# First group's products and masks by chunk, keys and scores in tiles of their own, and other orders in the opening and the first three turns

## The chip, the cores and the metric

The kernel runs on one core of one Trainium2 chip. The metric is the device time of one execution in microseconds (us), the median of several runs. Lower is better. A profile of one execution gives the times of single instructions.

## The reference, cut to what matters

```python
# gated linear attention: B, H, S, D = 4, 8, 768, 48
for t in range(S):
    state = alpha[:, :, t, :, None] * state + k[:, :, t] (outer) v[:, :, t]
    y[:, :, t] = q[:, :, t] @ state
x = y as (B, S, H*D)                                  # 4 x 768 x 384
# gated state-space block: d_inner = 512
proj = x @ w_in                                       # 384 x 1024
val, gate = proj[..., :512], proj[..., 512:]
h_t = a * h_(t-1) + val_t                             # a = exp(A_log), a scan over time
out = (silu(gate) * h) @ w_out                        # 512 x 384
```

The weights w_in and w_out arrive as 64-bit floats and are converted to 32-bit on the chip. q, k, v and alpha are 32-bit.

## The kernel before, in words

The sequence is cut into N = 12 groups of 256 steps (three for each of four batches). A group has two chunks (`c`) of 128 steps, and a chunk two halves of L = 64 steps; `u` counts the four blocks of 64. The order of all instructions is written out by hand (no scheduler): each engine, and each queue that issues DMAs, works its own list from front to back and waits for others by semaphores.

The attention of a group `m` goes in these steps:

- Products. alpha, q and k of the group are brought to a layout with the 48 dimensions on the partitions: for groups 0 to 2 by TensorE (`alphas`, `straighten`: 16 matmuls with the identity, and a ScalarE copy from PSUM, L648, L658, L663), from group 3 on by VectorE (`turn`, L576). `scan_P` (L602) scans the running product P of alpha, `scan_V` (L610 to L618) scans V, the inverse product, backwards. `scaled_q` (L585) writes q times P into `Zq`, `scaled_k` (L590) writes k times V into `Zk`. From group 3 on these steps are the generator `products`, whose seven steps are taken by `go(1)` and `go(2)` in between the steps of a turn. `junk` (L596) is a check on ScalarE that reads alpha.
- `scores(m)` (L684): for each half and head, one matmul of `Zk` against `Zq`. `Zq` holds the identity in its first 48 columns, so that the result has 48 columns that give the key back, by steps, and 64 columns that are scores. Chunk 0 goes to the PSUM tile `s`, chunk 1 to a tile `mm`.
- `masks(m)`: ScalarE copies the keys from PSUM into `AK` (L693; for one half of the heads the scores too), VectorE multiplies scores by the triangular mask into the same `AK` (L699), and GpSimd masks the other half (L696). For group 0 (`alone`) all four masks are VectorE's.
- `values(m)` (L714) multiplies the masked scores with v, `states(m)` (L741) the keys with v. ScalarE copies the states to `dS` (L746), GpSimd adds them up (`add_up`, L756 and L758, tile `sum`), and `carried` (L727) adds the part of earlier blocks to the PSUM tile `y`. For group 0 `carried_by_parts` (L767) does that from `dS` directly.
- `join(m)`: ScalarE copies `y` to `yst` (L788), eight DMAs move it to the rows of `xT` (L790), and two copies move the rest (L793).

The state-space block of a group `n` goes in `project(n, cc)` for cc = 0 to 3 (L806, six matmuls of 128x256 columns, VectorE's scan `hh` L809, ScalarE's `sg` L814, GpSimd's product `f` L815), and `output(n)` (L824, L828, L829). `convert(i)` makes 32-bit weights of the 64-bit ones, for i = 0 to 3 a quarter of w_in, for 4 and 5 a half of w_out: ScalarE's `low` (L525) and three VectorE operations (L534, L536, L538). `load_w` and `load_w_out` load the 64-bit weights.

The loop runs over turns n = 0 to 11. In turn n the state-space block of group n and the attention of group m = n + 1 are interleaved, and the products of group n + 2 go on VectorE. `first` is scores and masks, `second` is values, states and sums, `third` is the carried part, the other half of the values, and `join`. Pools matter: PSUM tiles `mm` come from a pool of two (projections, scores of chunk 1, outputs and transposes take turns), `s` and `y` have one each. `keep_warm` issues matmuls on zeros without a use for the result.

Of the kernel before, what the change touches and what calls it, by code (L numbers as in the profile page):

```python
# [345 lines left out]
def fast(  # L346
# [68 lines left out]
    def load_steps(name, m, engine):  # L415
# [49 lines left out]
    AK = [const.tile([C, G, 4, L + D], FP32, name=f"AK{i}") for i in range(2)]  # L465
    Zqs = [const.tile([C, 4, 2 * G, L + D], FP32, name=f"Zq{i}") for i in range(2)]
# [16 lines left out]
    def constants():  # L483
# [21 lines left out]
        for t in sums:  # L505
            nc.gpsimd.memset(t[:, :, D:64], 0.0)
        for t in Zqs:
            for i in range(2):
                rows = ds(64 * i, 64)
                nc.gpsimd.tensor_copy(out=t[rows, :, :, 0:D].rearrange("p h u d -> p (h u) d"),  # L510
# [69 lines left out]
    def plain(name):  # L580
        tag = "Zk" if name == "k" else "q"
        return (p2 if name == "k" else p1).tile([C, 4, GC], FP32, tag=tag, name=tag)

    def scaled_q(m, t, P):
        nc.vector.tensor_mul(Zqs[m % 2][:, :, :, D:], t.rearrange("p h (u t) -> p h u t", t=L),  # L585
                             P[:, :, 1:GP].rearrange("p h (u t) -> p h u t", t=L))

    def scaled_k(m, t, V):
        Zks[m] = t
        nc.vector.tensor_mul(t, t, V[:, :, 1:GP])  # L590

# [83 lines left out]
    def scores(m):  # L675
        Zk, Zq = Zks[m], Zqs[m % 2]
        scs[m] = [bank_pair("s"), bank_pair()]
        for c in range(G):
            for p in range(4):
                for h in range(2):  # L680
                    u = 2 * c + h
                    for i in range(2):
                        rows = ds(64 * i, D)
                        nc.tensor.matmul(scs[m][c][ds(L * h, L), i, ds(p * (L + D), L + D)],  # L684
                                         Zk[rows, p, ds(u * L, L)], Zq[rows, p, u],
                                         start=True, stop=True, skip_group_check=True)

    def masks(m, alone=False):
        sc = [t[:, :, 0:4 * (L + D)].rearrange("p i (h x) -> p i h x", h=4) for t in scs.pop(m)]
        for i in (1, 0):  # L690
            for c in range(G):
                n = L + D if i and not alone else D
                nc.scalar.activation(AK[i][:, c, :, 0:n], sc[c][:, i, :, 0:n], AF.Copy)  # L693
        if not alone:
            t = AK[1].rearrange("p c h x -> p (c h) x")[:, :, D:]
            nc.gpsimd.tensor_mul(t, t, mask[:, None, :].to_broadcast([C, G * 4, L]))  # L696
        for c in range(G):
            for i in range(2 if alone else 1):
                nc.vector.tensor_mul(AK[i][:, c, :, D:], sc[c][:, i, :, D:],  # L699
                                     mask[:, None, :].to_broadcast([C, 4, L]))  # L700

    def values(m, across):
# [4 lines left out]
        for c in range(G):  # L707
            for e in range(2):
                for h in range(2):
                    i = 1 - h if across else h  # L710
                    for s in range(2):
# [3 lines left out]
                                         v_sb[rows, c, 4 * i + p, :], AK[i][rows, c, p, D:],  # L715
# [303 lines left out]
```

## Time and profile before

| what | value |
|---|---|
| median of 3 runs | 299.87 us (298.01 to 300.7) |
| profiled execution, its own time | 299.45 us |
| its span | 297.6 us |
| TensorE matmul busy | 280.9 us (94%), 4062 instructions |
| VectorE busy | 210.3 us (71%) |
| ScalarE busy | 107.9 us (36%) |
| GpSimd busy | 118.4 us (40%) |
| mean granted TensorE clock | 0.98 |

PE is TensorE's matmul, PEld its weight load, DVE VectorE, ACT ScalarE, POOL GpSimd, SP SyncE, whose queue issues most DMAs. L12 is line 12 of the kernel. In the strips of the page the span is cut into 40 equal slices, and each digit is the busy share in tenths; PEclk is the clock that TensorE was granted, in tenths of full speed. A timeline row gives the start, the length, the engine, the line, the operation, the tiles, and in brackets the idle time before it with what ended it. The chain of waits is followed back from the last instruction.

### The profile page before, as it was taken

The numbers are of one execution on the slowest core, as the hardware profiler recorded it, in microseconds if no ns is written. First come the engines' busy times: TensorE is split into PE (matmuls) and PEld (weight loads), VectorE is DVE, ScalarE is ACT, GpSimd is POOL, SyncE is SP. The second block draws the span as 40 slices with busy tenths as digits, with TensorE's granted clock in tenths as the row PEclk, the third lists the DMA queues.
The fourth block names the chain that finished last, engine by engine and source line by source line (L and its number), as shares of the span: only waits on it lengthen the run. The fifth ranks groups of instructions, "written<-read, shape, count | busy, mean of one in ns | idle before, by whom it ended". The sixth has DMA issues, their size and how long they took to land.

```text
span 297.6 us, 9503 instructions
## 1 busy us (share of the span) xinstructions
PE 280.9 (94%) x4062; PEld 220.8 (74%) x4062; DVE 210.3 (71%) x233; ACT 107.9 (36%) x236; POOL 118.4 (40%) x139
## 2 busy tenths in 40 slices
PE   7997987879999999999999999999999999999991
PEld 5886876458868878778778688688687787786860
DVE  4879665948659959849859679598599598259420
ACT  1766446130532532433235144224315333331211
POOL 8001728314405626516318238146156174141110
PEclk9999998895999999999999999999999999999998
DMA  6990798634188197294394593791871921100101
GB/s 211 252 327 14 216 328 185 144 93 101 29 205 209 42 245 168 70 255 122 82 266 115 135 249 74 166 247 45 219 198 43 247 61 41 55 15 28 55 4 62
DMA packets 54180, 41.86 MB, mean 141 GB/s; under 512 B 29520, under 2 KB 52016, under 8 KB 54128
## 3 DMA queue, kind: packets, MB, share of 16 engines
q1 hardware_dynamic: 53184, 40.60, 52.5%
q8 instruction: 34, 0.56, 0.8%
q10 hardware_dynamic: 816, 0.40, 0.5%
q0 software_dynamic: 128, 0.16, 0.2%
q14 instruction: 18, 0.15, 0.2%
HBM read 32.88 MB, written 4.72 MB: 126 GB/s over the span
## 4 chain that ended last, share of the span: by engine, by line
PE 76%; DMA 6%; DVE 5%; POOL 4%; ACT 4%; issue 2%; SPq 1%; DVEq 0%; POOLq 0%; ACTq 0%
PE pvg L806 37%; PE o L824 18%; PE y L714 4%; PE y L727 4%; PE s L741 3%; PE mm L648 3%; PE s L684 3%; DMA wbits<-in_moe_w_in_dram 3%; POOL sum L758 3%; PE mm L684 2%; DMA raw_k<-in_k_dram 1%; DMA raw_a<-in_alpha_dram 1%; DVE hh L809 1%; POOL f L815 1%; ACT dS L746 1%
## 5 line engine op out<-in xcount | busy, mean ns | idle before, releaser
L806 PE MATMUL pvg<-xT,w_in 128*128 128x256 f32 x576 | 137.5, 393 | 1.0 <-DVE w_in L538 1.0
L806 PEld LDWEIGHTS pvg<-xT,w_in 128*128 128x128 f32 x576 | 109.1, 194 | 18.6 <-PE s L741 1.1
L815 POOL TENSOR_TENSOR f<-sg,hh 128x256 f32<-128x256 f32 x48 | 57.9, 1208 | 52.0 <-ACT sg L814 52.0
L824 PE MATMUL o<-w_out,f 128*128 128x384 f32 x192 | 64.4, 487 | 1.4 <-POOL f L815 0.8
L814 ACT ACTIVATE sg<-pvg 128x256 f32<-128x256 f32 x48 | 18.5, 385 | 112.3 <-DVE hh L809 88.5
L824 PEld LDWEIGHTS o<-w_out,f 128*128 128x128 f32 x192 | 36.5, 191 | 25.1 <-POOL f L815 1.4
L758 POOL TENSOR_TENSOR sum<-sum,dS 128x192 f32<-128x192 f32 x40 | 33.0, 824 | 28.7 <-ACT dS L746 26.8
L809 DVE TENSOR_TENSOR_SCAN hh<-a_dec,hh,pvg 128x256 f32<-128x256 f32 x32 | 23.2, 724 | 21.4 <-PE pvg L806 21.3
L696 POOL TENSOR_TENSOR AK<-AK,mask 128x512 f32<-128x512 f32 x11 | 14.0, 1272 | 57.9 <-ACT AK L693 57.9
L699 DVE TENSOR_TENSOR AK<-s,mask 128x256 f32<-128x256 f32 x13 | 5.4, 424 | 38.9 <-ACT AK L693 38.9
L602 DVE TENSOR_TENSOR_SCAN P<-al,lower 128x1028 f32<-128x1028 f32 x12 | 27.6, 2298 | 4.1 <-ACT al L658 4.0
L618 DVE TENSOR_TENSOR_SCAN V<-al,ends 128x1028 f32<-128x1028 f32 x12 | 27.9, 2328 | 0.1
L828 ACT ACTIVATE o_sb<-o 128x384 f32<-128x384 f32 x24 | 10.5, 488 | 47.0 <-PE o L824 47.0
L714 PE MATMUL y<-AK,v 64*64 64x64 f32 x768 | 16.9, 225 | 2.5 <-POOL AK L696 2.0
L714 PEld LDWEIGHTS y<-AK,v 64*64 64x64 f32 x768 | 14.0, 137 | 6.4 <-issue 4.2
L576 DVE STREAM_TRANSPOSE Zk<-raw_k 128x1024 f32<-128x1024 f32 x9 | 18.4, 2045 | 0.0
L576 DVE STREAM_TRANSPOSE al<-raw_a 128x1024 f32<-128x1024 f32 x9 | 18.4, 2042 | 0.0
L576 DVE STREAM_TRANSPOSE q<-raw_q 128x1024 f32<-128x1024 f32 x9 | 18.2, 2020 | 0.0
L727 PE MATMUL y<-Zq,sum 48*64 48x64 f32 x656 | 15.2, 223 | 1.8 <-issue 1.2
L727 PEld LDWEIGHTS y<-Zq,sum 48*64 48x64 f32 x656 | 12.3, 134 | 6.0 <-issue 3.7
L585 DVE TENSOR_TENSOR Zq<-q,P 128x1024 f32<-128x1024 f32 x12 | 14.7, 1221 | 0.4
L741 PE MATMUL s<-v,AK 64*64 64x48 f32 x704 | 14.2, 223 | 0.8 <-issue 0.8
(93 smaller groups left out, 274.0 us busy)
## 6 DMA issues: line engine op xcount, KB each, us to landing
v<-in_v_dram SPq DMA_DIRECT2D x24, 192.0 KB, 3.8
out_dram<-o_sb SPq DMA_DIRECT2D x24, 192.0 KB, 3.3
raw_a<-in_alpha_dram SPq DMA_DIRECT2D x18, 184.0 KB, 4.5
raw_k<-in_k_dram SPq DMA_DIRECT2D x18, 184.0 KB, 4.3
raw_q<-in_q_dram SPq DMA_DIRECT2D x18, 184.0 KB, 4.2
raw_a<-in_alpha_dram SPq DMA_DIRECT2D x18, 176.0 KB, 4.6
raw_k<-in_k_dram SPq DMA_DIRECT2D x18, 176.0 KB, 4.4
raw_q<-in_q_dram SPq DMA_DIRECT2D x18, 176.0 KB, 4.4
```

The costliest lines, as they stand in the source:

```text
L576: nc.vector.transpose(out=by_runs(to).rearrange("p h c j -> p h j c"), in_=raws[name][:, 0:4 * ROW].rearrange("p (h j d) -> p h j d", h=4, ...
L602: nc.vector.tensor_tensor_scan(out=P, data0=al[:, 0:4 * GP], data1=lower.rearrange("p h t -> p (h t)"), initial=0.0, op0=ALU.mult, op1=ALU ...
L618: nc.vector.tensor_tensor_scan(out=V[:, ::-1], data0=al[:, 1:4 * GP + 1][:, ::-1], data1=ends.rearrange("p h t -> p (h t)")[:, ::-1], init ...
L714: nc.tensor.matmul(ys[m][ds(64 * s, 64), i, e, ds(c * C + h * L, L)], v_sb[rows, c, 4 * i + p, :], AK[i][rows, c, p, D:], start=across and ...
L727: nc.tensor.matmul(ys[m][ds(64 * s, 64), i, e, ds(u * L, L)], Ss[j][rows, p, :], Zqs[m % 2][rows, p, u, D:], start=False, stop=True, skip_ ...
L741: nc.tensor.matmul(st[ds(64 * i, 64), h, c, p, :], AK[i][rows, c, p, 0:64], vs[m % NV][rows, c, 4 * i + p, 0:D], start=True, stop=True, sk ...
L758: nc.gpsimd.tensor_add(Ss[j][:, :, 0:D], Ss[j - 1][:, :, 0:D], part)
L806: nc.tensor.matmul(pj, w_ins[cc][:, kk, vg, :], xT[:, kk, :], start=(kk == 0), stop=(kk == NK - 1))
L809: nc.vector.tensor_tensor_scan(out=hh, data0=a_dec[:, cc:cc + 1].to_broadcast([C, GC]), data1=pv, initial=prev_h[cc][:, GC - 1:GC] if n % ...
L814: nc.scalar.activation(sg, pg, AF.Silu)
L815: return lambda: nc.gpsimd.tensor_mul(fs[n][:, cc, :], sg, hh)
L824: nc.tensor.matmul(os[c], fs[n][:, cc, ds(c * C, C)], w_outs[cc // 2][:, cc % 2, :], start=(cc == 0), stop=(cc == NI - 1))
```

## The change

Line numbers of the kernel after the change differ by some ten to twenty.

- `AK` becomes two kinds of tiles, `As` for masked scores and `Ks` for keys. `masks` copies keys and masks scores chunk by chunk, a key ahead of its score; for other groups than 0 GpSimd's half of the scores is copied first. `Ks` gets zeros in its last 16 columns from GpSimd at the start.
- `Zq` and `Zk` are laid out by chunk; k has a tile of its own from which `scaled_k` writes `Zk`. For group 0 `scaled_k` and `scaled_q` go chunk by chunk, behind `scan_V`.
- The first loads of alpha, q and k are split over SyncE's and ScalarE's queues. The second half of w_in is loaded ahead of the first scores instead of behind `join(0)`.
- Two of the zero matmuls are gone. In the opening, `scan_P(1)` stands behind the masks of group 0, `straighten(1, "k")` and `scan_V(1)` behind `join(0)`, `convert(0)` before it. `join(0)` issues its DMAs from GpSimd's and ScalarE's queues, and half of its copy is VectorE's.
- `straighten` of group 2 for k and q moves into turn 0, and `junk(2)` and the scans of group 2 move behind `convert(5)`.
- In turn 1, the first two projections stand before the scores; in turn 2, one projection. `carried` goes over blocks 0, 2, 3 in place of 2, 3, 0.

```diff
-            engine.dma_start(
+            engines[i % len(engines)].dma_start(
                 out=steps_of(name, m)[:, ds(i * ROW, ROW)],
...
-    AK = [const.tile([C, G, 4, L + D], FP32, name=f"AK{i}") for i in range(2)]
-    Zqs = [const.tile([C, 4, 2 * G, L + D], FP32, name=f"Zq{i}") for i in range(2)]
+    As = [const.tile([C, G, 4, L], FP32, name=f"A{i}") for i in range(2)]
+    Ks = [const.tile([C, G, 4, L], FP32, name=f"K{i}") for i in range(2)]
+    Zqs = [const.tile([C, 2 * G, 4, L + D], FP32, name=f"Zq{i}") for i in range(2)]
...
+    def scaled_q(m, t, P, c=None):
+        u0, n = (0, 2 * G) if c is None else (2 * c, 2)
+        at = ds(u0 * L, n * L)
+        nc.vector.tensor_mul(Zqs[m % 2][:, ds(u0, n), :, D:].rearrange("p u h t -> p h u t"),
...
+    def scaled_k(m, t, V, c=None):
+        if not c:
+            Zks[m] = p2.tile([C, G, 4, C], FP32, tag="Zk", name="Zk")
+        c0, n = (0, G) if c is None else (c, 1)
...
-        for i in (1, 0):
+        mb = mask[:, None, :]
+        if not alone:
             for c in range(G):
-                n = L + D if i and not alone else D
-                nc.scalar.activation(AK[i][:, c, :, 0:n], sc[c][:, i, :, 0:n], AF.Copy)
-        if not alone:
-            t = AK[1].rearrange("p c h x -> p (c h) x")[:, :, D:]
-            nc.gpsimd.tensor_mul(t, t, mask[:, None, :].to_broadcast([C, G * 4, L]))
+                nc.scalar.activation(As[1][:, c], sc[c][:, 1, :, D:], AF.Copy)
+            t = As[1].rearrange("p c h x -> p (c h) x")
+            nc.gpsimd.tensor_mul(t, t, mb.to_broadcast([C, G * 4, L]))
         for c in range(G):
-            for i in range(2 if alone else 1):
-                nc.vector.tensor_mul(AK[i][:, c, :, D:], sc[c][:, i, :, D:],
-                                     mask[:, None, :].to_broadcast([C, 4, L]))
+            for i in range(2):
+                nc.scalar.activation(Ks[i][:, c, :, 0:D], sc[c][:, i, :, 0:D], AF.Copy)
+                if alone or i == 0:
+                    nc.vector.tensor_mul(As[i][:, c], sc[c][:, i, :, D:], mb.to_broadcast([C, 4, L]))
...
-        for i in range(2):
-            nc.scalar.activation(st[:, i], y[:, i], AF.Copy)
+        nc.scalar.activation(st[:, 0], y[:, 0], AF.Copy)
+        if m == 0:
+            nc.vector.tensor_copy(out=st[:, 1], in_=y[:, 1])
+        else:
+            nc.scalar.activation(st[:, 1], y[:, 1], AF.Copy)
...
+    load_w(1, nc.sync)
     nc.scalar.activation(a_dec, a_log, AF.Exp)
     nc.scalar.activation(spare, minus, AF.Silu)
     P = scan_P(0)
-    scaled_q(0, tq, P)
     junk(0)
     V = scan_V(0, P)
-    scaled_k(0, tk, V)
-    keep_warm(2, 512)
+    for c in range(G):
+        scaled_k(0, tk, V, c)
+        scaled_q(0, tq, P, c)
     alphas(1)
     tq = straighten(1, "q", "y")
     junk(1)
     keep_warm(1, 512, "s")
     scores(0)
+    masks(0, True)
     P = scan_P(1)
-    masks(0, True)
-    tk = straighten(1, "k")
     low(0)
     values(0, True)
     states(0)
     low(1)
-    V = scan_V(1, P)
+    convert(0)
     carried_by_parts(0)
     values(0, False)
-    join(0, [nc.sync, nc.gpsimd])
+    join(0, [nc.gpsimd, nc.scalar])
+    tk = straighten(1, "k")
+    V = scan_V(1, P)
     scaled_q(1, tq, P)
     scaled_k(1, tk, V)
-    convert(0)
     convert(1)
-    load_w(1, nc.sync)
...
-    P = scan_P(2)
-    tk = straighten(2, "k")
-    tq = straighten(2, "q")
-    load_raw("a", 3, nc.sync)
-    load_v(2, nc.sync)
-    for name in "kq":
-        load_raw(name, 3, nc.sync)
...
-            carried(m, (2, 3, 0))
+            carried(m, (0, 2, 3))
...
             f1 = project(n, 1)
+            tk = straighten(2, "k")
+            load_raw("k", 3, nc.sync)
             second(m)
             f0()
             f1()
             convert(3)
-            junk(2)
             f2 = project(n, 2)
+            tq = straighten(2, "q")
+            load_raw("a", 3, nc.sync)
+            load_v(2, nc.sync)
+            load_raw("q", 3, nc.sync)
             third(m)
...
-            convert(5)
             f3 = project(n, 3)
             f3()
+            convert(5)
+            junk(2)
+            P = scan_P(2)
             V = scan_V(2, P)
...
-            if n > 1:
+            if n > 2:
                 first(m)
                 load_raw("q", n + 2, nc.sync)
                 go(1)
             f0 = project(n, 0)
             if n == 1:
+                f1 = project(n, 1)
                 first(m)
-                go(1)
-            second(m)
-            f0()
-            load_raw("a", n + 3, nc.sync)
-            go(2)
-            f1 = project(n, 1)
+                go(2)
+                second(m)
+                f0()
+                f1()
+                load_raw("a", n + 3, nc.sync)
+            else:
+                if n == 2:
+                    first(m)
+                    load_raw("q", n + 2, nc.sync)
+                    go(1)
+                second(m)
+                f0()
+                load_raw("a", n + 3, nc.sync)
+                go(2)
+                f1 = project(n, 1)
+                f1()
...
+            f2 = project(n, 2) if n == 1 else None
+            if n == 1:
+                go(1)
             third(m)
-            f1()
...
-            f2 = project(n, 2)
+            f2 = f2 or project(n, 2)
```

More of the change, by code (lines that the diff above doesn't have):

```diff
@@ L506, in constants @@
             nc.gpsimd.memset(t[:, :, D:64], 0.0)
+        for t in Ks:
+            nc.gpsimd.memset(t[:, :, :, D:], 0.0)
         for t in Zqs:
@@ L727, in carried @@
                         nc.tensor.matmul(ys[m][ds(64 * s, 64), i, e, ds(u * L, L)], Ss[j][rows, p, :],
-                                         Zqs[m % 2][rows, p, u, D:], start=False, stop=True,
+                                         Zqs[m % 2][rows, u, p, D:], start=False, stop=True,
                                          skip_group_check=True)
```

40 lines of the change are left out of this document (20 added, 20 removed).

## The prediction

> **What bounds the kernel now.** I read the page first, then the chain of waits, the timeline of the opening, and windows of 2 us for the clock. The page gives the shape:
>
> ```profile
> span 297.6 us, 9503 instructions
> ...
> PE   7997987879999999999999999999999999999991
> ...
> DVE  4879665948659959849859679598599598259420
> ...
> PEclk9999998895999999999999999999999999999998
> ...
> PE 76%; DMA 6%; DVE 5%; POOL 4%; ACT 4%; issue 2%; SPq 1%; DVEq 0%; POOLq 0%; ACTq 0%
> ```
>
> TensorE is full from the eleventh slice (74 us) on; what it loses lies before. From the first scores of turn n=3 (107.61 us in the timeline) a turn takes 20.8 us and TensorE sets it. So I ask when the changed kernel reaches that point, and whether its later turns stay 20.8 us. Two things decide. The first is the masks. In the opening:
>
> ```profile
> 17.68 1.14 ACT L596 ACTIVATE junk<-al,minus 128x1028 bf16<-128x1028 f32 x1
> ...
> 18.90 0.33 ACT L693 ACTIVATE AK<-s 128x192 f32<-128x192 f32 x1
> ...
> 20.31 0.76 DVE L699 TENSOR_TENSOR AK<-s,mask 128x256 f32<-128x256 f32 x2 [1.91 <-ACT AK L693]
> ```
>
> ScalarE copies all four keys, then VectorE masks: one hand-over, hidden by transposes on TensorE (19.54 to 21.5). The second is a chain that already touches TensorE in turn n=4 (start, length):
>
> ```profile
> 131.57 0.40 DVE AK L699
> 131.97 1.23 DVE al L576
> ...
> 133.77 0.68 DVE hh L809
> ...
> 134.93 0.61 ACT dS L746 x2
> ...
> 135.57 1.64 POOL sum L758
> ...
> 137.28 0.61 POOL sum L758
> ...
> 137.96 0.61 POOL sum L758
> ...
> 138.62 0.69 PE y L727 x32
> ```
>
> The masks release the turn of alpha, this hh, this sg and dS, and the sums release `carried`. The first sum takes 1.64 us against 0.61 for the next: the scan for P (134.51 to 136.81) runs beside it, and the sum ends 0.4 us after the scan. The same 0.4 us stands in turn n=3 (scan to 115.61, sum to 116.01).
>
> The clock is the third loss (us, then busy time of the five engines, granted clock, DMA):
>
> ```profile
> 66.00:68.00 2.00, 0.70 (x28) 0.70 (x32) 1.85 (x3) 0.34 (x2) 1.24 (x1) 0.84 0.00 0
> 68.00:70.00 2.00, 2.00 (x65) 1.91 (x58) 1.95 (x3) 0.00 (x0) 0.00 (x0) 0.50 0.04 11
> ```
>
> Values of turn n=1 wait 2.0 us for the POOL mask (65.3 to 67.3), and from 67.4 to 74.2 the clock is 0.50. There, values and states take 2.7 us against 1.8 in later turns, and a projection 4.9 against 2.8: about 3.3 us lost. An earlier stretch at 0.50 (50.3 to 53.7) follows waits of 0.3 and 1.2 us and makes the projection there 4.5: 1.7 us lost. Waits of 1.0 us (41.9) and 0.8 (58.6) were followed by none.
>
> **The change, step by step.** I follow the waits in the built programs and put in durations from rows of before.
>
> *Opening.* alpha of group 0 comes over two queues, so its transposes start when the warm-up ends (4.46) and not in pieces until 5.46: they end at 6.75 for 7.63, 0.9 earlier (bounds 0.3 and 0.9; the later the second half lands, the less). P runs 7.85 to 10.15; with `scaled_q` moved behind V, V runs 10.5 to 12.8; four half products (1024 columns take 1.23, half about 0.6) end at 15.3. Without the two 512-column warm-ups (1.9 us) TensorE has done alpha and q of group 1 at 14.0, the last warm-up at 15.0, scores at 16.75 for 19.61. That is 2.85 earlier. But ScalarE is not: junk(0) (1.2), alpha (1.03), q of group 1 (it waits for the last half product, 15.3), then junk(1), end at 17.5, so the first key starts at 17.5 for 18.90.
>
> *Keys and scores in their own tiles.* SBUF tiles are split, but both engines still read one PSUM tile, and the program orders them: key, score, key, score, each waiting for the other engine. With 0.33 and 0.42 and 0.04 per hand-over: 17.5, 17.85, 18.3, 18.7, and the last score at 20.3 for 21.73. The transposes that covered this are moved behind the group, so TensorE waits from 16.75 to 19.1 and 19.5 to 20.3. Then values, states (1.1), dS (0.65), parts (1.63), values (0.7) end y of group 0 at 24.75. Before, 1.36 us of instruction waits ("issue") lay in this stretch, and 3.2 us of waiting may halve the clock for one stretch (2.7 us more). I take 26.1, the middle of 24.75 and 27.5, for 27.66.
>
> *To the end of output(0).* xT of group 0 goes over GpSimd's and ScalarE's queues: four issues of 0.65 on ScalarE stand before its xT copies, its k copy and its alpha copy. First projection 31.1 to 33.9 (it waits for that k copy) for 35.84; scores(1) end at 35.7 for 37.5. The first half gives 1.8 so far. Loading w_in's second half earlier removes the 1.0 us before project(0,2) (convert(2) waited for a DMA until 40.08). Against it, k and q of group 2 (3.8 us of transposes) now stand among the projections, as before they stood ahead of them. project(0,1) waits for sg(0,0), which waits for hh behind convert(1); k's transposes wait for the last key copy; third(1) ends at 48.75 for 49.44. convert(4) needs its ScalarE half, queued behind yst and xT: done 52.45. convert(5), now behind hh(0,3) and sg(0,3): 55.55 for 55.67. So TensorE waits 0.9 and 1.8 us inside output(0) and ends it at 59.5. That much waiting in 4 us is more than what preceded the stretch at 50.3, so I add the 1.7 of that stretch: 61.2 for 61.0. Term +0.2 (bounds -1.5, with no stretch, and +1.5, with y of group 0 at 27.5).
>
> *Turn n=1.* Two projections stand before scores(2); the scan for P and V of group 2, moved behind convert(5), finish the products at 62.8, which the two projections (to 66.8) cover. Uncovered they would hold scores from 61.2, 1.6 us. Then masks as before: the first POOL mask can start 0.16 earlier, since ScalarE copies 256 columns (0.39) and not 448 (0.55). Term -0.2, with a stretch of half clock as in before.
>
> *Turn n=2.* Before, scores(3) stood ahead of project(2,0), which covered the masks (88.7 to 91.4). Now scores(3) stand behind it and values(3) right behind the scores: the wait of turn n=1 comes a second time. Term +1.8, bounds 1.8 and 5.1 (with 3.3 of half clock). The two waits are equal; the clock changed at 50.3, 53.7, 67.4 and 74.2, all multiples of 3.4 us apart, so a wait of 1.8 us falls whole into one such period in about half the cases. I count one stretch for the two.
>
> *Turns n=3 to 10.* ScalarE and VectorE alternate here too. From the end of scores: before, the last mask ended 1.6 us later (130.36, 131.97). Now score copies end at +0.45, then key to +0.67, mask to +1.12, key, key to +1.7, mask to +2.2. The turn of alpha starts 0.56 later, with it P's scan, the first sum and `carried`. Slack of TensorE was 0.2 us in n=4, 7, 10, 0.4 in n=3, 6, 9, 0.6 in n=5, 8, and putting the last group's carry first covers another 0.23 ahead of the third sum. Left are about 0.33, 0.2 and 0.25 a turn: 2.1, I take +2.0. Bounds: -0.7 (the 0.23 is all that shows, in three turns) and +4.5 (all 0.56 in eight). What else is in these turns is covered: ScalarE's 0.35 us more per turn lie in 9 us of idle, and sg(n,2) still ends 0.5 us before output needs its bank.
>
> *Sum.* +0.2 - 0.2 + 1.8 + 2.0 = +3.8 on the profiled execution's 299.45 (span 297.6 and 1.85 around it): 303.25. The median 299.87 is 0.42 above that execution, so 303.7.
>
> **Rivals.** *The clock stays full.* For it: waits of 0.8 and 1.0 us left it alone, the weight load is earlier and two projections run into turn n=1. Against it: 2.0 us did not, and the walk has 3.2, 2.7, 1.8 and 1.8. It decides at the wait before output(0): without the stretches (1.7 and 3.3) and the half clock in the opening (1.35) the time is 303.7 - 6.4 = 297.3, under before; own range 293 to 299. The Trainium skill, page "TensorE: Matmul & The Clock Gate", section "HAM oscillation — how this bites in real kernels", asks only for no gap over about 3.4 us; by that rule none of these waits would cost clock, and the trace disagrees (2.0 us, then 0.50). *One more stretch*, at turn n=2: 303.7 + 3.3 = 307.0. For it: the same wait was followed by 0.50 in before. Against: phase. *The alternation costs nothing later*: if sums hide the 0.56 us, 301.7. For it: n=5 and 8 have slack; against: the chain shown above. That the split does not free VectorE from ScalarE is part of the forecast.
>
> **Chances.** Forecast 0.40 (own range 301.5 to 306), clock full 0.25, one more stretch 0.17, no later cost 0.18. A measurement tells about 1% (3.0 us) from no change. Faster by more: 0.7 of clock full, 0.18. Within: 0.10 of the forecast, 0.145 of no later cost, the rest of clock full, 0.32. Slower by more: 0.50. The range 295 to 309 cuts the fast end of clock full and the sum of all upper bounds.
>
> **What would show it.** Right: key and mask rows alternate at 17.5 to 20.3; scores end near 16.8 and y of group 0 near 26; PE rows wait 0.9 and 1.8 us on w_out; turn n=2 has a wait of 1.8 on the POOL mask; from n=3, P's scan starts 0.5 later after the scores, and turns take 21.0 to 21.1 us. Wrong: masks on VectorE back to back, turns of 20.8, clock 1.0 throughout, or the first scores of n=3 before 107.

## The result, and the profile after

The changed kernel takes 307.66 us (median; 307.09 to 311.08) against 299.93 us for the kernel before on the same chip: a ratio of 1.029, 95% interval 1.020 to 1.038. It is 7.7 us slower, where 3.8 us were forecast; 307.7 lies above the forecast's own range of 301.5 to 306. The profiled execution took 307.17 us, its span is 305.4 us. The page of the changed kernel, in the lines that were shown of before:

```profile
span 305.4 us, 9510 instructions
...
PE   7968899697997999999999999999999999999990
...
DVE  4856965877967859949849859678599499259310
...
PEclk9985999999997999999999999999999999999998
...
PE 65%; DVE 11%; DMA 7%; ACT 5%; issue 5%; POOL 4%; SPq 1%; DVEq 0%; ACTq 0%; POOLq 0%
```

The chain that ended last lies on TensorE for 65% of the span and no longer for 76%. What it lost went to VectorE (5% to 11%), "issue" (2% to 5%), ScalarE and DMA. The clock strip has its 5 in the fourth slice (22.9 to 30.5 us), in the first group, where before had full clock.

Where the 7.8 us between the two spans lie is read from the first `scores` row of each turn and the last matmul of `output(0)`. Turn n=2 of the changed kernel starts with its first projection, since its scores now stand behind that.

| point | before | after | difference | term measured | term forecast |
|---|---|---|---|---|---|
| `output(0)` ends | 61.0 | 63.4 | +2.4 | +2.4 | +0.2 |
| turn n=2 starts (scores; after: projection) | 86.94 | 87.49 | +0.55 | -1.85 | -0.2 |
| turn n=3 starts (first scores) | 107.61 | 111.74 | +4.1 | +3.6 | +1.8 |
| turn n=10 starts | 254.27 | 261.17 | +6.9 | +2.8 | +2.0 for n=3 to 10 |
| last matmul | 291.1 | 298.0 | +6.9 | 0.0 | |
| end | 297.6 | 305.4 | +7.8 | +0.9 | |

**The opening.** One timeline row each of ScalarE (ACT), VectorE (DVE) and TensorE (PE) in the changed kernel: start, length, instruction, and the idle time before it with its releaser.

```profile
18.15 0.32 ACT L708 ACTIVATE K<-s 128x192 f32<-128x192 f32 x1
18.57 0.42 DVE L710 TENSOR_TENSOR A<-s,mask 128x256 f32<-128x256 f32 x1 [2.57 <-ACT K L708]
19.03 0.33 ACT L708 ACTIVATE K<-s 128x192 f32<-128x192 f32 x1 [0.56 <-DVE A L710]
...
19.87 0.57 PE L724 MATMUL y<-A,v 64*64 64x64 f32 x16 [2.28 <-DVE A L710]
```

Key and score alternate, each waiting for the other engine, although their SBUF tiles are split. TensorE waits 2.28 us for the first masks and then 0.59 for the last. Windows of 2 us after that (length, then busy time of PE, PEld, DVE, ACT and POOL, granted clock, DMA share, GB/s):

```profile
20.00:22.00 2.00, 1.41 (x52) 1.23 (x55) 1.60 (x3) 1.11 (x2) 0.00 (x0) 0.52 1.13 343
...
28.00:30.00 2.00, 2.00 (x20) 1.65 (x16) 1.55 (x5) 0.39 (x1) 1.31 (x3) 0.50 1.01 349
```

From 20.1 to 30.3 us TensorE has half its clock, three periods of 3.4 us. From 24 to 34 us the DMA engines are full besides (share 0.88 to 1.01), where before they stood at 0.00 to 0.33 from 24 to 32. SyncE's queue tells why. Its rows in the kernel before, and then in the changed kernel:

```profile
28.35 3.07 SPq L790 DMA_DIRECT2D xT<-yst  x4
31.47 1.11 SPq L445 DMA_DIRECT2D wbits<-in_moe_w_in_dram  x2
32.63 1.21 SPq L451 DMA_DIRECT2D wobits<-in_moe_w_out_dram  x2
```

```profile
20.26 3.47 SPq L445 DMA_DIRECT2D wbits<-in_moe_w_in_dram  x2
23.78 1.23 SPq L451 DMA_DIRECT2D wobits<-in_moe_w_out_dram  x2
```

Before, the transfers of `xT` stood in SyncE's queue and waited for `yst`, and 3 MB of weights waited behind them. Now `xT` goes over other queues, nothing holds SyncE, and the weights of both matrices are under way when `xT` starts. One row of the DMA issues of that stretch, before and then after (the last figure is the median of the two transfers, in us from issue to landing):

```profile
xT<-yst POOLq DMA_DIRECT2D x2, 48.0 KB, 2.0
```

```profile
xT<-yst POOLq DMA_DIRECT2D x2, 48.0 KB, 5.3
```

**Turns n=1 and n=2.** TensorE waits for GpSimd's mask in both turns. The values of turn n=1, the values of turn n=2 and the projection that follows these:

```profile
72.14 0.77 PE L724 MATMUL y<-A,v 64*64 64x64 f32 x30 [1.84 <-POOL A L705]
...
93.78 0.78 PE L724 MATMUL y<-A,v 64*64 64x64 f32 x30 [1.84 <-POOL A L705]
...
95.66 4.29 PE L819 MATMUL pvg<-xT,w_in 128*128 128x256 f32 x12
```

The clock is 1.00 in turn n=1 and 0.50 from 95.2 to 98.6 us, behind the second of the two waits.

**The turns from n=3 on** are 21.1 to 21.5 us long, and before 20.7 to 21.2. First the turn of alpha in turn n=4 of the kernel before (scores start at 128.59), then rows of VectorE, GpSimd and TensorE of the changed kernel (scores start at 133.04), which answer to the chain shown of before at 131.57 to 138.62:

```profile
131.89 2.04 DVE L576 STREAM_TRANSPOSE al<-raw_a 128x1024 f32<-128x1024 f32 x1
```

```profile
136.55 0.42 DVE L710 TENSOR_TENSOR A<-mm,mask 128x256 f32<-128x256 f32 x1 [0.62 <-ACT K L708]
136.90 2.04 DVE L579 STREAM_TRANSPOSE al<-raw_a 128x1024 f32<-128x1024 f32 x1
...
140.46 3.12 POOL L768 TENSOR_TENSOR sum<-sum,dS 128x192 f32<-128x192 f32 x3 [3.85 <-ACT dS L756]
...
142.26 0.46 PE L737 MATMUL y<-Zq,sum 48*64 48x64 f32 x16 [0.35 <-POOL sum L768]
```

The turn of alpha starts 3.86 us after the scores, before 3.30. The sums end as much later, and TensorE waits 0.35 us for them.

### The profile page after: what moved, and what is told of

Read it like the earlier page. It is cut to its first block, busy times and chain, and to the rows that moved or that the text cites. A ratio compares the mean times of both kernels' runs of the same rounds, so it can differ in the third digit from the quotient of the medians.

```text
span 305.4 us, 9510 instructions
## 1 busy us (share of the span) xinstructions
PE 281.7 (92%) x4058; PEld 221.8 (73%) x4058; DVE 214.3 (70%) x236; ACT 111.0 (36%) x257; POOL 117.5 (38%) x141
## 4 chain that ended last, share of the span: by engine, by line
PE 65%; DVE 11%; DMA 7%; ACT 5%; issue 5%; POOL 4%; SPq 1%; DVEq 0%; ACTq 0%; POOLq 0%
PE pvg L819 29%; PE o L837 19%; DMA out_dram<-o_sb 5%; PE y L737 3%; PE s L694 3%; POOL sum L768 3%; PE y L724 2%; PE mm L658 2%; DVE al L579 2%; DVE hh L822 2%; DMA raw_a<-in_alpha_dram 2%; PE s L751 2%; DVE P L612 2%; DVE V L628 1%; PE mm L694 1%
## 5 line engine op out<-in xcount | busy, mean ns | idle before, releaser
L819 PE MATMUL pvg<-xT,w_in 128*128 128x256 f32 x576 | 135.5, 388 | 1.1 <-ACT al L668 1.1
L819 PEld LDWEIGHTS pvg<-xT,w_in 128*128 128x128 f32 x576 | 107.6, 192 | 18.9 <-issue 1.7
L828 POOL TENSOR_TENSOR f<-sg,hh 128x256 f32<-128x256 f32 x48 | 54.6, 1139 | 48.3 <-ACT sg L827 48.3
L705 POOL TENSOR_TENSOR A<-A,mask 128x512 f32<-128x512 f32 x11 | 14.0, 1269 | 65.2 <-ACT A L703 65.2
L710 DVE TENSOR_TENSOR A<-s,mask 128x256 f32<-128x256 f32 x13 | 5.5, 425 | 36.1 <-ACT K L708 36.1
L724 PE MATMUL y<-A,v 64*64 64x64 f32 x768 | 17.4, 228 | 6.6 <-POOL A L705 3.7
L724 PEld LDWEIGHTS y<-A,v 64*64 64x64 f32 x768 | 14.5, 140 | 10.2 <-POOL A L705 4.1
L579 DVE STREAM_TRANSPOSE k<-raw_k 128x1024 f32<-128x1024 f32 x9 | 18.4, 2046 | 0.0
L598 DVE TENSOR_TENSOR Zk<-k,V 128x1024 f32<-128x1024 f32 (+1 forms) x13 | 16.1, 1237 | 0.3
L589 DVE TENSOR_TENSOR Zq<-q,P 128x1024 f32<-128x1024 f32 (+1 forms) x13 | 14.9, 1148 | 0.3
```

Source lines behind the costliest of these rows:

```text
L579: nc.vector.transpose(out=by_runs(to).rearrange("p h c j -> p h j c"), in_=raws[name][:, 0:4 * ROW].rearrange("p (h j d) -> p h j d", h=4, ...
L598: nc.vector.tensor_mul(Zks[m][:, ds(c0, n)].rearrange("p c h t -> p h c t"), t[:, :, at].rearrange("p h (c t) -> p h c t", t=C), V[:, :, 1 ...
L724: nc.tensor.matmul(ys[m][ds(64 * s, 64), i, e, ds(c * C + h * L, L)], v_sb[rows, c, 4 * i + p, :], As[i][rows, c, p, :], start=across and ...
L819: nc.tensor.matmul(pj, w_ins[cc][:, kk, vg, :], xT[:, kk, :], start=(kk == 0), stop=(kk == NK - 1))
L828: return lambda: nc.gpsimd.tensor_mul(fs[n][:, cc, :], sg, hh)
```

## Experiments

All ratios are against the kernel before, run on the same chip. "Periods" are the periods of 3.4 us at half clock in the profiled execution (all lie before 102 us).

| run | median us | ratio (95% interval) | span | periods |
|---|---|---|---|---|
| before | 299.9 | | 297.6 | 3 |
| changed kernel | 307.7 | 1.029 (1.020 to 1.038) | 305.4 | 4 |
| e1_no_alt | 304.6 | 1.018 (1.012 to 1.024) | 305.3 | 6 |
| e2_scores3_first | 304.3 | 1.021 (1.014 to 1.029) | 302.5 | 3 |
| e3_filled | 307.9 | 1.029 (1.022 to 1.036) | 306.2 | 4 |
| e4_split_alone | 302.4 | 1.015 (1.008 to 1.021) | 300.0 | 1 |
| e5_convert5_first | 308.1 | 1.028 (1.021 to 1.035) | 307.6 | 6 |
| e6_join_sync | 306.5 | 1.022 (1.016 to 1.027) | 306.2 | 6 |
| e7_w_in_late | 307.4 | 1.028 (1.024 to 1.032) | 305.3 | 3 |
| e8_turn1_alone | 297.2 | 0.994 (0.990 to 0.997) | 294.3 | 1 |
| e9_repaired | 296.3 | 0.992 (0.988 to 0.996) | 294.3 | 3 |
| e10_turn1_low4 | 297.5 | 0.994 (0.990 to 0.998) | 295.4 | 1 |
| e11_repaired_filled | 296.7 | 0.990 (0.985 to 0.994) | 294.9 | 1 |
| e12_repaired_actq | 300.4 | 1.001 (0.998 to 1.004) | 296.6 | 3 |

The intervals are up to 0.9% to either side, so single edits of 1 us are read from the rows and not from the medians. A period at half clock takes at most 1.7 us, and their number differs between kernels that are alike there, so a span is compared only together with its periods.

### Is it the alternation that makes the later turns long? (e1, e4)

```diff
         for c in range(G):
             for i in range(2):
                 nc.scalar.activation(Ks[i][:, c, :, 0:D], sc[c][:, i, :, 0:D], AF.Copy)
-                if alone or i == 0:
+                if alone:
                     nc.vector.tensor_mul(As[i][:, c], sc[c][:, i, :, D:], mb.to_broadcast([C, 4, L]))
+            if not alone:
+                nc.vector.tensor_mul(As[0][:, c], sc[c][:, 0, :, D:], mb.to_broadcast([C, 4, L]))
```

> The changed kernel, but from group 1 on ScalarE copies both keys of a PSUM tile before VectorE masks its score (group 0 as changed). Theory, the alternation makes the sums late in every later turn: turns n=3 to n=9 go from 21.3-21.5 back to 20.8-21.0, the alpha turn starts 3.3 us after the scores and not 3.86, and the kernel ends 3.0 to 3.7 us earlier, at about 304.3. Rival, the other order of the turn (f(n,1) and sg(n,1) ahead of the carry, last group's carry first) makes the turns long: turns stay 21.3-21.5 and the time stays within 0.7 us of 307.7.

Measured: the turns n=3 to 9 are 20.98, 21.14, 20.71, 20.92, 21.14, 20.71 and 20.93 us, and from turn n=3 to turn n=10 it is 146.5 us, against 149.4 in the changed kernel and 146.7 before. Rows of VectorE and TensorE of e1 in turn n=4 (scores at 135.79):

```profile
139.27 2.04 DVE L579 STREAM_TRANSPOSE al<-raw_a 128x1024 f32<-128x1024 f32 x1
...
144.63 0.46 PE L739 MATMUL y<-Zq,sum 48*64 48x64 f32 x16
```

The turn of alpha starts 3.48 us after the scores, 0.38 earlier than in the changed kernel, and the carry has no wait in front of it. The whole 2.8 us of these seven turns is the alternation; the order of f1 and of the carry, which e1 keeps, costs nothing there. (The profiled execution's span is no shorter than the changed kernel's because it had six periods at half clock. It was the slowest of its four, 307.06 us; the others took 303.2 to 305.0.)

e4 does that part of the change alone, on the kernel before: the tiles `As` and `Ks`, the whole of the changed `masks`, and nothing else.

```diff
-    AK = [const.tile([C, G, 4, L + D], FP32, name=f"AK{i}") for i in range(2)]
+    As = [const.tile([C, G, 4, L], FP32, name=f"A{i}") for i in range(2)]
+    Ks = [const.tile([C, G, 4, L], FP32, name=f"K{i}") for i in range(2)]
...
```

> The kernel before with one part of the change alone: keys and scores in tiles of their own, with the masks in the changed order (key, score, key, score). Theory: the turns from n=3 take 21.2 to 21.4 as in the changed kernel, 0.3 to 0.5 longer each over nine turns, so 3.0 to 3.7 us more, about 303.3; in the opening the transposes still cover the masks. Rival, the alternation costs nothing without the new order of the turn: 299.9, turns of 20.8.

Measured: turns of 21.1, 21.5 and 21.7 us from n=3 on, 150.2 us for the seven, 3.6 more than before; the median is 3.0 us over before. So this part alone makes the kernel slower. Of its 3.6 us the whole change has 2.8, so its order gives back 0.8 in these turns. In the rows of e4's turn n=4 the carry waits twice, 0.34 us for the first sum and 0.20 us before its last blocks; in the changed kernel, with the order 0, 2, 3, only the first wait is left.

### Turn n=2 (e2)

```diff
-            if n > 2:
+            if n > 1:
                 first(m)
...
-                if n == 2:
-                    first(m)
-                    load_raw("q", n + 2, nc.sync)
-                    go(1)
                 second(m)
```

> The changed kernel with the scores of turn n=2 ahead of project(2,0), as before the change. Theory: the 1.84 us wait on the GpSimd mask goes, and with it the stretch of half clock at 95.6 to 98.9 that follows it (1.5 us in project(2,1)): 3.4 us less, about 304.3. Rival 1, the clock's stretch belongs to the wait of turn n=1 and only comes later: 1.8 us less, 305.9. Rival 2, the first sum (beside the scan for P) is late as well and holds the carry: under 1 us less, 307.

Measured: 304.3 us, as the theory said. TensorE in turn n=2:

```profile
89.56 2.86 PE L819 MATMUL pvg<-xT,w_in 128*128 128x256 f32 x12
92.35 0.69 PE L724 MATMUL y<-A,v 64*64 64x64 f32 x32
```

The projection runs through to the values with no wait, and the clock stays at 1.00 in all of turn n=2 (changed kernel: 0.50 from 95.2 to 98.6, project(2,1) 4.29 us long and not 2.86). Turn n=3 starts at 109.02 and not at 111.74, 2.7 us earlier. New waits of 0.42 us (for VectorE's products, ahead of the scores) and 0.21 (for the sums) take up the rest of the 3.4.

### The opening: half clock, queues and the chain to output(0) (e3, e6, e7, e5)

```diff
     scores(0)
+    keep_warm(2, 512)
     masks(0, True)
```

> The changed kernel with two 512-column matmuls on zeros (0.95 us each) behind scores(0), in the 2.28 us wait for the first masks. Theory, that wait halves the clock from 20 to 30 us: the clock stays 1.00 there, y of group 0 ends at 25 and not 27.7; the first projection starts 1.5 to 2.5 us earlier, and since convert(4) is queued behind yst of group 1 on ScalarE, output(0) follows by 1 to 2: 305.7 to 306.7. Rival, the time of the first group is not what sets output(0), which waits for the conversions of w_out (VectorE's own 14 us of products, conversions and hh): y of group 0 is early, the waits before output(0) grow by as much, and the time stays at 307.7. Second rival: the clock falls at 20 all the same, and y ends at 27.7.

Measured: 307.9 us, the time of the first rival, but not for its reason. The filling does to the clock what it should: 1.00 until 31.0 us, and y of group 0 ends at 25.4 and not 27.7. But TensorE stops for 3.25 us in the transposes of k (26.5 to 29.7, put down to "issue"), the clock falls after that stop, `xT` lands 5.9 to 6.8 us after its issue, and scores(1) start at 37.75 against 37.76. The gain was lost between y of group 0 and the first projection, and not, as the rival had it, in the waits before `output(0)`, which are 1.08 and 1.91 us as in the changed kernel.

```diff
-    join(0, [nc.gpsimd, nc.scalar])
+    join(0, [nc.sync, nc.gpsimd])
```

> The changed kernel with the eight transfers of xT of group 0 over SyncE's and GpSimd's queues, as before the change, and none over ScalarE's. Theory 1, the 2.78 us of issues on ScalarE (28.41 to 31.19) hold its k copy and alpha copy, and with them the first projection: the projection starts at 31.5 to 32.5 and not 34.48, scores(1) end 2 us earlier, output(0) up to 1.5 earlier, 306.2. Theory 2, which the trace favours: TensorE's transposes of k and alpha end at 31.65 and 33.4 whatever ScalarE does, and the copies follow them: the projection starts at 34.0 to 34.5 and the time stays within 0.5 us of 307.7.

Measured: 306.5 us, and neither theory was right in its reasons. `xT` lands in 1.9 to 2.9 us and not 5.2 to 5.7 (medians of its pairs of transfers), the first projection starts at 33.30 and scores(1) at 36.50, 1.3 us earlier. ScalarE's issues were not what held it: its copy of k still follows the transposes (31.68). What changed is that w_out now stands behind `xT` in SyncE's queue. The changed kernel's wait of 1.08 us ahead of the first projection is put down to ScalarE's copy of alpha, but in e6 the projection starts at 33.30, before that copy ends (34.49). So the wait was for `xT`, whose transfers landed from 34.1 us on. But `output(0)` ends only 0.4 us earlier. hh(0,0) stands behind convert(1) on VectorE and starts at 37.90 (37.87 in the changed kernel), so TensorE waits 0.79 us for sg(0,0) ahead of the second projection and most of the gain is gone.

```diff
     load_v(1, nc.sync)
-    load_w(1, nc.sync)
...
     convert(1)
+    load_w(1, nc.sync)
```

> The changed kernel with the second half of w_in loaded where the kernel before loads it, behind convert(1). Theory, the early load only takes away a wait of 1.0 us ahead of project(0,2), which the waits before output(0) give back: the time stays within 0.7 us of 307.7, convert(2) waits for its transfer, and TensorE's unexplained stop in the transposes of k (0.72 us at 30.05) stays or goes without an effect on output(0). Rival, the load takes transfer time from the first group: its absence lets the transposes run through and xT land earlier, and the first projection starts 0.7 or more earlier: 306.7. Other rival: without it convert(2) is late by 2 us or more and output(0) with it: 309.5.

Measured: 307.4 us. The edit did not do what it was meant to: SyncE has nothing to wait for in this kernel, so it issued the same load at 19.67, as early as before the edit (20.26). What it shows is the queue again: `xT` lands after 6.5 to 7.0 us, and the first projection waits 3.68 us, put down to the DMA of `xT`, and starts at 34.87. Whether an early second half of w_in is worth anything is left open by it.

```diff
+            convert(5)
             f3 = project(n, 3)
             f3()
-            convert(5)
             junk(2)
```

> The changed kernel with convert(5) ahead of project(0,3), so that hh(0,3) and sg(0,3) stand behind it and not ahead. Theory, the order on VectorE makes the 1.91 us wait inside output(0): convert(5) ends at 58.3 and not 59.16, the wait falls to about 1.0, the last part of output(0) waits for f(0,3) instead, output(0) ends 0.9 earlier at 62.5: 306.8. Rival, convert(4) is what is late (its ScalarE half stands behind yst and the xT copies, 2.98 us of waiting on VectorE) and hh(0,3) becomes late by as much as convert(5) is early: 307.7, no change.

Measured: 308.1 us. The wait inside `output(0)` falls from 1.91 to 1.03 us as the theory said, a third one of 0.39 us for f(0,3) takes a part of it back, and the profiled execution had two more periods at half clock than the changed kernel (in turn n=1). From the scores of group 1 to the end of `output(0)` it is 25.4 us, and 25.7 in the changed kernel: the edit is worth 0.2 us, and the rival is right.

### Versions put together (e8, e9, e10, e12, e11)

Turn n=1 of the kernel before, alone in another order:

```diff
             f0 = project(n, 0)
             if n == 1:
                 first(m)
                 go(1)
+                f1 = project(n, 1)
             second(m)
...
-            f1 = project(n, 1)
+            if n == 1:
+                f1()
+                f2 = project(n, 2)
+            else:
+                f1 = project(n, 1)
+                f2 = None
...
             third(m)
```

> The kernel before, with turn n=1 alone in another order: project(1,1) between scores(2) and values(2), project(1,2) ahead of the carry. Theory: project(1,1) covers the masks, the 2.0 us wait goes and with it the two periods of half clock at 67.4 to 74.2 (3.3 us): 294 to 295. Rival 1, the clock falls elsewhere in the turn: 297.4. Rival 2, the sums (late beside the scan for P) hold the carry and give the 2.0 us back: 299.4.

Measured: 297.2 us, ratio 0.994 (0.990 to 0.997). TensorE of e8 in turn n=1:

```profile
65.72 2.86 PE L806 MATMUL pvg<-xT,w_in 128*128 128x256 f32 x12
68.51 0.69 PE L714 MATMUL y<-AK,v 64*64 64x64 f32 x32
```

No wait, no half clock, and the turn is 19.2 us from scores to scores and not 23.4; 0.4 us before scores(3) are a new wait for VectorE's products. The profiled execution gains 3.3 us, the medians 2.0.

e9 puts six orders of the changed kernel right, those of e1, e2 and e5 and three that the diff shows, and has `join(0)` as in e6. (Its expectation says that `join(0)` stays on ScalarE's queue; the kernel that ran had it over SyncE's and GpSimd's.)

```diff
+    V = scan_V(1, P)
-    join(0, [nc.gpsimd, nc.scalar])
+    join(0, [nc.sync, nc.gpsimd])
     tk = straighten(1, "k")
-    V = scan_V(1, P)
...
+            low(4)
             third(m)
...
             f0 = project(n, 0)
             if n == 1:
-                f1 = project(n, 1)
                 first(m)
                 go(2)
+                f1 = project(n, 1)
                 second(m)
```

> The changed kernel with seven orders put right at once: the three of e1, e2 and e5 (both keys of a tile before its score; scores(3) ahead of project(2,0); convert(5) ahead of project(0,3)), V of group 1 ahead of join(0) on VectorE, so that it doesn't wait 2.7 us behind the copy of y, ScalarE's half of convert(4) ahead of third(1), scores(2) between project(1,0) and project(1,1), and w_in early as it is, join(0) over ScalarE's queue as it is. Theory, the losses add up: 307.7 less 3.3 (turns) less 3.4 (turn n=2) less 1.8 (turn n=1) less 1.0 to 2.5 (output(0)) gives 296.7 to 298.2. Rival, the transfers of xT beside w_out's hold the first projection whatever VectorE does, and the gains at output(0) don't come: 299 to 300. Other rival: the waits closed in the opening are followed by others, and stretches of half clock stand in their place: 301 or more.

Measured: 296.3 us, ratio 0.992 (0.988 to 0.996): 11 us faster than the changed kernel and faster than before. Scores(1) start at 36.09, the wait before `output(0)` is gone, `output(0)` ends at 59.3 (before 61.0), and the turns from n=2 on are 20.7 to 21.2 us.

e12 undoes in e9 only the queues of `join(0)`:

```diff
-    join(0, [nc.sync, nc.gpsimd])
+    join(0, [nc.gpsimd, nc.scalar])
```

> The kernel of e9 with one part as in the change: xT of group 0 over GpSimd's and ScalarE's queues, so that SyncE's loads of w_out no longer wait behind it. Theory, w_out's transfers fill the engines while xT is under way: xT lands 5 to 6.5 us after its issue and not 1.9 to 3.0, DMA is at 1.00 from 28 to 32 and not 0.31, the first projection starts 1.5 to 3.5 us later (34.2 to 36), and the time is 1.0 to 2.5 more than e9's: 297.3 to 298.8. Rival, ScalarE's issues and the transfers lie beside the transposes and VectorE's work: within 0.7 of 296.3.

Measured: 300.4 us, ratio 1.001 (0.998 to 1.004) against e9's 0.992 (0.988 to 0.996): 0.9% for one line. The two ran on different chips; e11, which differs from e9 only by two filling matmuls, ran on the same chip as e12 and took 296.7 us. The theory's mechanism holds, and its price of 1.0 to 2.5 us is too low by the medians (3.7 us from e11 to e12). SyncE's queue and the first projection in e9, and then the first projection in e12:

```profile
28.16 2.53 SPq L805 DMA_DIRECT2D xT<-yst  x4
30.74 2.32 SPq L451 DMA_DIRECT2D wobits<-in_moe_w_out_dram  x2
...
32.64 1.13 PE L821 MATMUL pvg<-xT,w_in 128*128 128x256 f32 x4
```

```profile
34.30 3.22 PE L821 MATMUL pvg<-xT,w_in 128*128 128x256 f32 x12 [1.41 <-DVE Zk L598]
```

In e9 w_out waits behind `xT`, in e12 it is issued at 22.54. `xT` lands after 1.9 to 3.0 us in e9 and after 5.2 to 5.6 us in e12 (medians of its pairs of transfers), the DMA share from 28 to 32 us is 0.31 and 1.01, and the first projection starts at 32.64 and 34.30. (The row's releaser is VectorE's Zk, whose row at 32.61 lasts 1.50. But in e9 the projection starts at 32.64 while Zk runs until 33.44, so it does not need Zk. What it waits for is `xT`, whose transfers land between 33.9 and 35.5 us in e12.) Both profiled executions had three periods at half clock, in the same place; the spans differ by 2.3 us.

e11 is e9 with the two filling matmuls of e3.

> The kernel of e9 with the two 512-column matmuls on zeros of e3 behind scores(0). (In e9 xT of group 0 went over SyncE's and GpSimd's queues, with w_out behind it, not over ScalarE's as its expectation says.) Theory: with xT's transfers in 1.9 to 3.0 us the group's time does reach the first projection, so what e3 could not show is seen here: the clock stays 1.00 from 19.6 to 29.8, y of group 0 ends at 25 and not 27.4, the first projection starts at 30.5 to 31.5 and not 32.64, and the time is 1.0 to 2.0 less than e9's: 294.3 to 295.3. Rival, a stretch of half clock follows the next wait and VectorE's products and conversion set the first turn: within 0.7 of 296.3.

Measured: 296.7 us, ratio 0.990 (0.985 to 0.994): no difference to e9 that can be told. The clock is 1.00 until 28.4 and y of group 0 ends at 25.0, as in e3, and again TensorE stops on its way to the projection:

```profile
28.48 0.91 PE L658 MATMUL mm<-ident,raw_k 128*64 128x128 f32 x6 [2.49 <-issue]
```

The first projection starts at 32.90, in e9 at 32.64. So the half clock of the first group can be removed, but nothing was gained by it in two kernels.

e10 is e8 with three things more: `low(4)` ahead of `third(1)`, the second half of w_in ahead of group 0's scan, and the carry 0, 2, 3.

> The kernel before with the new order of turn n=1 (as in e8), ScalarE's half of convert(4) ahead of third(1), the second half of w_in loaded ahead of group 0's scan, and the last group's carry first (0, 2, 3). Theory: the waits of 0.6 and 0.8 us before and inside output(0) and the 0.8 us on w_in go, and 0.2 us in each of turns n=4, 7, 10 (21.0 for 21.19): 297.2 less 2.5, 294.5. Rival 1, hh(0,3) and sg(0,3) set the end of output(0) in any case, and only the turns gain: 296. Rival 2, the early w_in is in the way of xT of group 0 and the first projection comes later by what is gained: 297.

Measured: 297.5 us, ratio 0.994 (0.990 to 0.998), as e8: rival 2 by its size. Scores(1) start at 39.98 and not at 36.60: alpha of group 0 came later (TensorE waits 1.0 us for it), TensorE stops 1.64 us in the values of group 0 ("issue"), and a period at half clock follows. The wait on w_in falls from 0.83 to 0.35 us, but the waits for w_out are now 0.55 and 1.63 us. The turns do show the carry's order: n=4 takes 20.96 us for 21.20, though n=5 takes 21.27 for 20.68.

## Why the prediction was right or wrong

**The direction** was right, and so were the mechanisms of the opening's masks, of turn n=2 and of the later turns. The size was half, and the time lies above the forecast's own range. Four terms, one by one:

**Opening to output(0): +0.2 forecast, +2.4 measured, outside its bounds of -1.5 to +1.5.** The alternation was as forecast: waits of 2.28 and 0.59 us for 2.35 and 0.8, keys and scores in turn from 18.15 to 20.97 for 17.5 to 20.3. The scores ended at 17.59 for 16.75, since the transposes of alpha took 2.95 us for the 2.3 assumed and the last half product ended at 16.0 for 15.3. Two steps failed:

- "3.2 us of waiting may halve the clock for one stretch": it did for three, 20.1 to 30.3, and y of group 0 ended at 27.7, for 26.1 and an upper bound of 27.5. e3 and e11 show that the wait is what sets it off, and also that this alone is not worth time.
- "First projection 31.1 to 33.9": it ran from 34.48 to 37.8. The prediction counted ScalarE's issues of `xT`, and not the queue that `xT` had left. SyncE no longer waited, so w_out's load went ahead of `xT` and shared the DMA engines with it. e6, e7 and e12 show this. Put back alone, the queue is worth 1.3 us at scores(1) (e6); in the repaired order it is worth 2.3 us of the span (e9 against e12). VectorE's wait of 2.7 us for y ahead of V of group 1, which the new order brought, was not counted either. It delays convert(1), which ends at 37.6 in the changed kernel, where hh(0,0) then waits 0.24 us for the projection; in e6, where the projection is early, convert(1) is what holds hh(0,0).

The waits inside `output(0)` were forecast at 0.9 and 1.8 us and measured 1.08 and 1.91:

```profile
55.87 1.53 PE L837 MATMUL o<-w_out,f 128*128 128x384 f32 x4 [1.08 <-DVE w_out L541]
59.31 4.11 PE L837 MATMUL o<-w_out,f 128*128 128x384 f32 x12 [1.91 <-DVE w_out L541]
```

The order of VectorE and ScalarE was read rightly, but everything stands 3.3 to 3.6 us later (convert(4) done 55.72 for 52.45, convert(5) 59.16 for 55.55). The 1.7 us of half clock added there did not come; that error hid a part of the other. (Of the two waits from which it was taken, 0.3 and 1.2 us, the first is 0.42 by its row.)

**Turn n=1: -0.2 forecast, -1.85 measured.** The wait for the GpSimd mask is there (1.84 us). The clock stayed full after it, where the forecast put the two periods of before. In e3, e5 and e6, whose turn n=1 is the same, two periods came, in e2 and e7 none. The last section's grid of 3.41 us sorts these runs: in e3, e5 and e6 TensorE stands without a matmul for 1.70 to 1.84 us within one period of it, while in the changed kernel a border at 71.3 us cuts the wait into 0.99 and 0.85 us (e7: 0.96 and 0.89; e2: 1.38 and 0.47). Where the border falls differs from trace to trace, so most of this term was luck of the profiled execution.

**Turn n=2: +1.8 forecast, +3.6 measured, within its bounds of 1.8 and 5.1.** The wait of 1.84 us came as worked out, and one period at half clock after it (95.2 to 98.6). "One stretch for the two" was the right count for n=1 and n=2 together: it fell in n=2. The two terms together were +1.6 in the forecast and +1.7 measured. e2 shows that the order alone makes the wait, and that without the wait there is no period. The period does not always follow: e7 has the same wait of 1.84 us in turn n=2, and its clock stays full.

**Turns n=3 to 10: +2.0 forecast, +2.8 measured in n=3 to 9 and nothing in n=10, within the bounds of -0.7 and +4.5.** The shift of 0.56 us was right to the hundredth (3.30 to 3.86), and for n=4 and 7 so was the loss (0.33 us). Mis-sized were n=3, 6, 9 (0.32 to 0.34 for 0.2) and n=5, 8 (0.72 and 0.41 for 0.25), because the slack that was to take up the shift was counted too large. e4, which has the shift without the new order, shows it: its turns n=3, 4, 6, 7 and 9 are 0.54 to 0.57 us longer than before, and n=5 and 8 are 0.41 longer, so of 0.2 to 0.6 us of slack only up to 0.15 was there. The carry's new order gives back 0.21 to 0.23 us in those five turns, as credited, and nothing in n=5 and 8. In n=5 a stop of 0.41 us ("issue") in the middle of the carry came on top. Turn n=10, for which 0.33 was counted, takes 20.8 us on TensorE in both kernels: it has no turn of alpha to be shifted, since there is no further group. The last 0.9 us lies behind the last matmul, which comes 6.6 us before the end in the kernel before and 7.5 us in the changed one. In e9 and e12, whose code is the same there, it is 6.5 and 7.6 us, so it is spread and not the change.

**The rivals.** "The clock stays full" is refuted: four periods. "One more stretch" gave 307.0, near the 307.7, and its stretch in turn n=2 is there, but its two of turn n=1 are not; the time agrees because the opening cost 2.2 us more. "The alternation costs nothing later" is refuted by e1 and e4. The rule of the Trainium skill (page "TensorE: Matmul & The Clock Gate", section "HAM oscillation — how this bites in real kernels"), by which only gaps over about 3.4 us matter, would have given no half clock after any of these waits. The trace disagrees: the 2.28 us of the opening and the 1.84 us of turn n=2 were each followed by 0.50.

## What to carry to other kernels

A transfer that waits in a queue also holds back everything behind it, so whoever moves it to another queue must ask what is let loose: here 1.5 MB of w_out, in the way of 0.29 MB that the next step needed, and 0.9% of the time for one line. Splitting an SBUF tile doesn't free two engines that read one PSUM tile; let one engine take all that it needs from the tile before the other starts. Give masks on other engines a projection's length of TensorE work as cover (e2, e8): a wait of 1.8 us costs itself and often a period at half clock, depending on where the grid described below cuts it.

## What the runs showed that was not expected

**The clock goes in periods of one grid.** In the fourteen traces, all changes of the clock lie on a grid of 3.41 us, whose phase differs from trace to trace. Up to 115 us, 36 periods at full clock have 1.48 us or more without a matmul; 27 of them are followed by a period at 0.50. None of those with 1.43 us or less is. Of the nine that are not followed, eight lie between 54 and 63 us, in and before `output(0)`, where what runs are matmuls on the full 128x128 array; in most of the others the matmuls are of 64x64 and 48x64. The ninth is the wait of turn n=2 in e7 (1.73 us in its period). The way back fits this in part: the period from 67.4 to 70.8 us in the kernel before is busy throughout, mostly with values and states, and another at 0.50 follows; the period from 95.2 to 98.6 in the changed kernel is mostly a projection, and full clock follows. But in e5 the period from 24.6 to 28.0 us is busy with 128 matmuls of 48x64 and 64x64 alone, and full clock follows too. That small matmuls count for less is argued from this and was not tried. The Trainium skill, page "TensorE: Matmul & The Clock Gate", section "What's actually happening", gives the window as 3413 ns and free-running, and the traces agree with both.

**TensorE stops for nothing that the profile shows.** In the stretch from 26 to 31.4 us it stood still for 0.72 us in the changed kernel, 3.25 in e3, 2.49 in e11, 1.87 in e5 and 1.64 in e10, in the middle of a row of equal matmuls, with the DMA engines full before it; in all but the first a packet of the instruction queue began in the stop or in the microsecond before it. In e9, where the DMA share is 0.20 to 0.42 from 28 to 32 us, the stop was 0.29 us. Full DMA engines alone don't make it: e12 stops for 0.49 us, e2 for 0.42 and e7 not at all, with shares of 0.96 to 1.04 from 26 to 32 us. Late instructions would explain it. The Trainium skill, page "Runtime: NRT & Kernel Launch", section "Instruction fetch mechanics", has instructions come in blocks of 16 KiB by DMA, with the cost mostly hidden; if late instructions are the cause, it was not hidden here. No run took this apart, so it stays open.
